# Asking for the first expert's weights during the recurrence, in a gated linear attention followed by a top-2 mixture of experts

## The chip, the core and the metric

The kernel runs on one core of one Trainium2 chip. The metric is device time in microseconds (us); the time of a kernel is the median of its runs. Engines are named as in the profile: PE is the matmul engine (PEld its weight loads), DVE the vector engine, ACT the scalar engine, POOL is GpSimd, and SP the engine whose queue issues most of the transfers here.

## The reference

An attention recurrence over 4 batches, 8 heads, 768 steps and a head dimension of 48, and then a router with 8 experts over the 3072 rows of 384 that it makes:

```python
for t in range(S):
    state = alpha[:, :, t, :, None] * state + einsum('bhd,bhe->bhde', k[:, :, t], v[:, :, t])
    y[:, :, t] = einsum('bhd,bhde->bhe', q[:, :, t], state)
x = y.transpose(0, 2, 1, 3).reshape(3072, 384)
noisy = x @ w_gate + log1p(exp(x @ w_noise)) * noise
top2 = the two largest of each row; top2_w = their softmax
for each expert e, and each row that chose it with weight w:
    out[row] += w * (relu(x[row] @ w1[e]) @ w2[e])      # w1: 384 x 1024, w2: 1024 x 384
```

## The kernel before, in words

All of it is in f32. The first stage is the recurrence, in 24 chunks of 128 rows (6 to a batch); the second is the experts, in 24 pairs of tiles of 128 rows (256 rows for one expert), with three small tiles between them. The order of the instructions on every engine is written out by hand, inside `tc.manual_schedule()`.

**The recurrence.** The loop over n (L1460) runs 23 times, for chunks 0 to 22. Each turn first queues transfers on SP: v of chunk n+2, alpha of n+5, k and q of n+4, and `put_y(n-2)`, which writes finished rows into `x_rows` in DRAM (L1470). Then come 14 pieces in the order ORDER, each for a chunk one to three ahead or behind: transposes of alpha, k and q on PE (`alphas`, `keys`, `queries`, L338), running products on DVE, `scores` (L417), `output` (L461 and L254, whose result ACT copies to yT, L465), and `turn_y(n-1)` (L277), which multiplies yT into rows and router logits, copied by ACT into `y_sb` (L282). Between the pieces, `route` deals out the steps of the router for the six chunks of a unit, and `put_some` writes the chosen rows into `table` in DRAM by indirect transfers of POOL (L169). After the loop, chunk 23 still lacks its `output` and `turn_y`.

**The experts.** A pair goes through: `load_tab` (its part of the table, L1073), `load_w1` and `load_w2` (L946 and L948, 1536 KB each, on SP), `find_rows` on DVE (L1096 to L1108), `gather` (two indirect transfers of POOL from `x_rows` into `x_in`, L936), `turn_x` (six transposes on PE, L1118, copied by ACT to xt, L1119), `sum_x`, `sum_w1` and `sum_w2` on DVE (sums and differences of tiles, so that fewer products are needed, L1124 and L1127), 11 products of the first layer (L1180), 7 of the second (L1187), then `combine` and the indirect write into `out` (L929). Pairs 0 to 7 take the experts 0 to 7 in turn; they need only the rows of the first two units (chunks 0 to 11), so the router's work for units 2 and 3 runs beside them.

**What sets the order.** Each step of pair i has a time, T*i + t with T = 20, and `beside()` adds further steps with times of their own: what is left of the last chunks, of the router and of the table's puts. All are sorted by time (L1410), and the sorted list is the order in which every engine gets its instructions; a time has no other meaning. A pair's first product has t = 0. For the first two pairs EARLY_0 and EARLY_1 replace times by others. Steps with times under -1 are played inside the last turns of the recurrence: `until(t)` runs all steps up to t, and the line

```python
for at, place, t in ((3, 5, -301.0), (3, 9, -300.0), (2, 1, -199.0), (1, 1, -101.0), (1, -1, -100.0)):
    if n == LAST - at:
        chunk.insert(place, lambda t=t: until(t))
```

puts it into turn 23 - at, ahead of piece number `place`. All else follows the loop, in `until(1e9)`.

**Buffers and queues.** w1 and w2 have two buffers each. The two of w1 are used before by `by_chunk` (the router's noise, until turn 2) and `nothing` (zeros to clear the table, until turn 2). SP starts its transfers in the order of the program; each waits for its buffer, for the data, and for the transfer that used its semaphore before, eight places back. POOL's indirect transfers go through a queue of their own.

Of the kernel before, what the change touches and what calls it, by code (L numbers as in the profile page):

```python
# [18 lines left out]
def kernel(  # L19
# [137 lines left out]
    def nothing_in(on):  # L157
        nothing = on.tile([C, KO * F], F32, tag="w1", name="nothing")[:, 0:TROWS // C * 4]
        nc.vector.memset(nothing, 0.0)
        nc.vector.memset(nothing.rearrange("p (r w) -> p r w", w=4)[:, :, 0:1], float(NONE))  # L160
        return nothing

    def clear_table(nothing):
        entries.clear()
        cleared = nc.scalar.dma_start(out=table.bitcast(F32).rearrange("(p r) w -> p (r w)", p=C), in_=nothing)
        entries.append(cleared.ins)
# [48 lines left out]
    def load_router(on):  # L215
        w_r = on["one"].tile([C, NP, 2, E], F32, name="w_r")
        nc.gpsimd.memset(w_r, 0.0)
        place_ident()
        for w, src in enumerate((moe_w_gate, moe_w_noise)):
            for i, part in enumerate(src.rearrange("(j i d) e -> i d j e", i=2, d=D)):  # L220
                nc.sync.dma_start(out=w_r[ds(DP * i, D), :, w, :], in_=part)
        return w_r, load_noise(on)

    def place_router(w_r):
        for odd in range(2):
            nc.gpsimd.tensor_copy(
                out=to_rows.rearrange("p (j o) c -> p j o c", o=2)[:, :, odd, ds((1 - odd) * 2 * D, 2 * E)],
                in_=w_r.rearrange("p (j o) w e -> p j o (w e)", o=2)[:, :, odd])
# [6 lines left out]
    def turn_noise(by_chunk, on):  # L235
        tp = on["tp"].tile([C, E, NT], F32, tag="tp", name="tp")
        for e in range(E):
            nc.tensor.transpose(tp[:, e, :], by_chunk[:, e, :], ident[0:NT, 0:NT])
        nc.scalar.copy(noise.rearrange("p n e -> p e n"), tp)
# [538 lines left out]
    def put_some(n):  # L778
        for place, entry in to_put[:n]:
            put_entries(place, entry)  # L780
        del to_put[:n]
# [262 lines left out]
    def pairs(on):  # L1044
# [180 lines left out]
        def put_pair(i):  # L1225
            for s in range(2):
                put_tile(prev[i % 2][:, s], wheres[i][:, s, 0:1])

        T = 20.0
        EARLY_0 = {"tab": -301.0, "w1": -300.0, "find": -200.0, "gather": -199.0, "w2": -101.0, "turn": -100.0,  # L1230
                   "sum_x": -1.0, "s0": -0.9, "s1": -0.8, "s3": -0.7, "s2": -0.6, "t0": 3.5, "t1": 4.3}
        EARLY_1 = {"tab": -301.0, "find": -0.5, "gather": -0.4, "w1": 0.5, "w2": 5.0}

        def steps(i):
            w = lambda f, a: w1_(i, f, a)
# [2 lines left out]
            after = 3.5 if i > E and divmod(i - E, 2) in [(g, 1) for g in AFTER_GROUP] else 0.0  # L1238
            early = {0: EARLY_0, 1: EARLY_1, E: {"find": T * E - 21.5, "gather": T * E - 21.0}}.get(i, {})
            at = lambda name, t: early.get(name, T * i + t) - T * i  # L1240
# [141 lines left out]
    with ExitStack() as es:  # L1382
        on = pools(es, "")
        shared = on["one"].tile([C, 2 * (NP * (C + 1) + 1) + 4 * NP * C], F32, name="shared")
        (load, load_v, alphas, no_more, products, inverses, keys, scaled_keys, queries, scores, masked, turn_k,
         state, block, output, turn_y, put_y, route, route_on, all_routed, out_of_range, places) = fast_gla(on)
        pair_steps, clear_pairs, T = pairs(on)
        half_steps, clear_halves = small_tiles(on, places, shared)
        LAST = NT - 1
        PUTS = (5.0, 6.3, 7.6, 11.0, 12.3, 16.4, 17.7, 19.0)  # L1390

        def beside():

            at = (-0.95, 4.75, 3.66, 5.25, 6.9, 28.5)
            left = [(at[0], lambda: put_y(LAST - 2)), (at[1], lambda: output(LAST)), (at[2], lambda: turn_y(LAST - 1)),
                    (at[3], lambda: turn_y(LAST)), (at[4], lambda: put_y(LAST - 1)), (at[5], lambda: put_y(LAST)),
                    (6 * T + 5.5, lambda: out_of_range(0)), (6 * T + 18.7, lambda: out_of_range(1))]
            r1, r2, r3 = (5.5, 17.4, 18.7)
            when = lambda *steps: [d * T + t for d, t in steps]
            left += [(t, lambda: route_on(2)) for t in when((0, r2), (0, r2), (0, r3), (1, r1), (1, r2), (1, r3), (2, r1), (2, 12.9), (2, r2))]  # L1400
            left += [(t, lambda: route_on(3)) for t in when((2, r3), (2, r3), (3, r1), (3, r2), (3, r3), (4, r1), (4, r2), (5, 2.9), (5, r1))]
            left += [(t, lambda: route_on(3)) for t in when(*[(8, 3.5), (8, 15.0), (8, r2), (8, r3), (10, 3.5), (10, 15.0), (10, r2), (10, r3)])]
            puts = when(*[(d, t) for d, ts in ((2, (17.7, 19.0)), (3, PUTS), (4, PUTS[:2]), (5, PUTS[1:4] + PUTS[1:]), (6, PUTS[:2]))
                          for t in ts])
            left += [(t, lambda: put_some(1)) for t in puts]
            assert len(puts) == 4 * UC
            return left
# [6 lines left out]
        def until(t):  # L1414
            while work and work[0][0] <= t:
                work.pop(0)[1]()
# [6 lines left out]
        def warm(times):  # L1423
            for _ in range(times):
                nc.tensor.matmul(on["y"].tile([C, NP, C], F32, tag="y", name="y")[:, 0, :], ones, ones, start=True, stop=True)

        with tc.manual_schedule():
            load(0)
            load(1, "a")
            load_v(0)  # L1430
            load(1, "kq")
            warm(3)
            alphas(0)
            products(0)
            inverses(0)
            keys(0)
            scaled_keys(0)
            queries(0)
            alphas(1)
            products(1)  # L1440
            inverses(1)
            load(2)
            warm(2)
            scores(0)
            keys(1)
            no_more(0)
            scaled_keys(1)
            masked(0)
            turn_k(0)
            queries(1)  # L1450
            load_v(1)
            load(3)
            held.extend(load_router(on))
            alphas(2)
            no_more(1)
            load(4, "a")
            state(0)
            products(2)
            no_more(2)
            for n in range(LAST):  # L1460
                pieces = {"keys": lambda: keys(n + 2), "inverses": lambda: inverses(n + 2),
                          "scaled": lambda: scaled_keys(n + 2), "alphas": lambda: alphas(n + 3),
                          "turn_y": lambda: turn_y(n - 1), "turn_k": lambda: turn_k(n + 1),
                          "queries": lambda: queries(n + 2), "products": lambda: products(n + 3),
                          "no_more": lambda: no_more(n + 3), "block": lambda: block(n), "output": lambda: output(n),
                          "state": lambda: state(n + 1), "scores": lambda: scores(n + 1),
                          "masked": lambda: masked(n + 1)}
                names = (FIRST_ORDER if n == 0 else ORDER).split()
                assert sorted(names) == sorted(pieces)
                pieces = [lambda: (load_v(n + 2), load(n + 5, "a"), load(n + 4, "kq"), put_y(n - 2))] + \  # L1470
                    [pieces[name] for name in names]
                chunk = [lambda piece=piece, place=place: (piece(), route(n, place)) for place, piece in enumerate(pieces)]
                last = [lambda: put_some(3)]
                if n == 0:
                    chunk.append(lambda: place_router(held.pop(0)))
                if n == 1:
                    last.append(lambda: held.append(nothing_in(on["two"])))
                if n == 2:
                    chunk.append(lambda: clear_table(held.pop()))
                if n == 2:  # L1480
                    last.append(lambda: (clear_pairs(), clear_halves()))
                if n == 3:
                    last.append(place_slots)
                if n == 2:
                    chunk.insert(NOISE_AT, lambda: turn_noise(held.pop(0), on))
                for at, place, t in ((3, 5, -301.0), (3, 9, -300.0), (2, 1, -199.0), (1, 1, -101.0), (1, -1, -100.0)):
                    if n == LAST - at:
                        chunk.insert(place, lambda t=t: until(t))
                for piece in chunk + last:
                    piece()  # L1490

            until(1e9)
            assert not to_put and all_routed()
# [43 lines left out]
```

## Time and profile before

| | |
|---|---|
| median of 3 runs | 673.34 us (672.64 to 673.82) |
| the profiled execution: its time | 707.68 us |
| its span, first to last instruction | 706.0 us |
| mean granted clock of PE | 0.973 |
| PE busy | 665.5 us, 94% of the span |
| DVE, ACT, POOL busy | 458.5, 271.2, 313.0 us |
| moved by DMA | 105.63 MB, 150 GB/s on average |
| last `scores` of the recurrence on PE | starts at 159.40 us |
| first product of the first pair on PE | starts at 163.28 us |
| last matmul | ends at 697.0 us |

A line of the timeline gives start and duration in us, the engine, the line of the kernel, the operation, the tile written and the tile read, and in brackets how long the engine stood idle before it and what ended that. "SPq" is the queue of SP; the duration there is that of issuing a transfer, not of moving the data. A line of the windows gives, for a stretch of time, the busy time of PE, PEld, DVE, ACT and POOL with the number of their instructions, the granted clock of PE, the share of the DMA engines' time that is used, and GB/s. Names leave buffer numbers out, so both weights are called `w<-in_moe_w_dram`; L946 is a w1 and L948 a w2.

### The profile page before, as it was taken

How to read it: one execution, taken by the hardware profiler on the slowest of the kernel's cores; microseconds unless marked ns; L12 is line 12 of the kernel's file. 1: busy time of each engine (PE TensorE's matmuls, PEld its weight loads, DVE VectorE, ACT ScalarE, POOL GpSimd, SP SyncE). 2: the span in 40 equal slices, each digit the busy share in tenths (PEclk: the TensorE clock that was granted, in tenths of full speed). 3: DMA queues.
4: the chain of work that ended last, by engine and by line, in shares of the span. 5: the costliest groups of instructions: out<-in, count | busy, mean ns of one | idle time of the engine just before them, and what ended most of it. 6: DMA issues, size and time to landing. Idle time of an engine off the chain costs nothing. (4 is left out here: it accounts for less than half of the span.)

```text
span 706.0 us, 14849 instructions
## 1 busy us (share of the span) xinstructions
PE 665.5 (94%) x5605; PEld 636.4 (90%) x5605; DVE 458.5 (65%) x1081; ACT 271.2 (38%) x582; POOL 313.0 (44%) x420
## 2 busy tenths in 40 slices
PE   8999999998999697976999999999999999999994
PEld 6898899998999597975999999999999999998894
DVE  8678889876787465753658677646575565756532
ACT  4666676653433223312233333323333333333320
POOL 5252784873225633672341433443354234641231
PEclk9999999999999888996999999999999999999998
DMA  9998889849555453572520438427453364720111
GB/s 155 161 199 147 143 137 184 151 134 369 193 190 193 129 176 117 173 207 56 216 70 23 165 107 294 143 67 271 155 171 125 123 225 141 249 67 17 45 54 44
DMA packets 144181, 105.63 MB, mean 150 GB/s; under 512 B 109255, under 2 KB 131410, under 8 KB 144100
## 3 DMA queue, kind: packets, MB, share of 16 engines
q1 hardware_dynamic: 131716, 80.37, 44.0%
q0 software_dynamic: 12240, 23.80, 10.8%
q8 instruction: 47, 0.77, 0.5%
q10 hardware_dynamic: 144, 0.41, 0.1%
q14 instruction: 34, 0.28, 0.1%
HBM read 94.99 MB, written 14.86 MB: 156 GB/s over the span
## 5 line engine op out<-in xcount | busy, mean ns | idle before, releaser
L936 POOL DMA_INDIRECT x_in<-x_rows,where x48 | 53.0, 1104 | 170.0 <-PE h_ps L1187 82.4
L1180 PE MATMUL sc<-xs,ws 128*128 128x128 f32 x576 | 76.5, 283 | 4.8 <-ACT m L1258 2.0
L929 POOL DMA_INDIRECT out_dram<-prev,where x48 | 50.9, 1060 | 61.1 <-DVE prev L1208 38.5
L1180 PEld LDWEIGHTS sc<-xs,ws 128*128 128x128 f32 x576 | 70.7, 197 | 6.4 <-ACT m L1258 2.8
L1180 PE MATMUL sc<-xt,w 128*128 128x128 f32 x576 | 75.8, 284 | 0.0
L1180 PEld LDWEIGHTS sc<-xt,w 128*128 128x128 f32 x576 | 73.0, 201 | 0.0
L1191 ACT ACTIVATE h<-h 128x512 f32<-128x512 f32 x72 | 45.4, 631 | 69.8 <-DVE h L1127 69.5
L921 POOL DMA_INDIRECT prev<-out_dram,where x48 | 52.6, 1097 | 43.3 <-DMA out_dram<-prev,where 22.3
L1187 PE MATMUL o_ps<-wt,hx 128*128 128x192 f32 x384 | 70.3, 326 | 0.0
L1127 DVE TENSOR_TENSOR h<-sc,m 128x512 f32<-128x512 f32 x48 | 33.1, 691 | 55.9 <-PE sc L1180 46.2
L1187 PEld LDWEIGHTS o_ps<-wt,hx 128*128 128x128 f32 x384 | 63.7, 190 | 0.0
L169 POOL DMA_INDIRECT table<-entry,place_u x48 | 53.8, 1120 | 15.8 <-issue 15.1
L1180 PE MATMUL sc<-xs,w 128*128 128x128 f32 x384 | 50.9, 287 | 4.3 <-DVE h L1127 4.3
L1180 PEld LDWEIGHTS sc<-xs,w 128*128 128x128 f32 x384 | 46.3, 197 | 7.8 <-DVE h L1127 6.3
L396 POOL TENSOR_TENSOR k_P<-k_P,over 128x512 f32<-128x512 f32 (+1 forms) x25 | 28.9, 1158 | 43.0 <-DVE over L378 17.6
L1180 PE MATMUL h_ps<-xt,w 128*128 128x128 f32 x384 | 47.7, 278 | 0.0
L1196 ACT ACTIVATE o<-o_ps,tab 128x192 f32<-128x192 f32 x23 | 9.6, 419 | 98.3 <-PE o_ps L1187 81.4
L338 PE MATMUL tp<-ident,ins 128*128 128x128 f32 x288 | 43.4, 286 | 3.1 <-DMA ins<-in_alpha_dram 1.8
L1180 PEld LDWEIGHTS h_ps<-xt,w 128*128 128x128 f32 x384 | 45.5, 194 | 0.1
L1127 DVE TENSOR_TENSOR h<-h_ps,m 128x512 f32<-128x512 f32 x24 | 16.6, 690 | 43.8 <-PE h_ps L1180 25.1
L1180 PE MATMUL sc<-xt,ws 128*128 128x128 f32 x192 | 29.2, 298 | 12.8 <-issue 12.8
L422 DVE COPY_PREDICATED shared<-upto,sc 128x512 f32<-128x512 uint32 x48 | 32.5, 733 | 13.3 <-PE sc L417 13.0
(257 smaller groups left out, 1440.3 us busy)
## 6 DMA issues: line engine op xcount, KB each, us to landing
w<-in_moe_w_dram SPq DMA_DIRECT2D x30, 1536.0 KB
ins<-in_alpha_dram SPq DMA_DIRECT2D x24, 192.0 KB
ins<-in_k_dram SPq DMA_DIRECT2D x24, 192.0 KB
ins<-in_q_dram SPq DMA_DIRECT2D x24, 192.0 KB
vt<-in_v_dram SPq DMA_DIRECT2D x24, 192.0 KB
x_rows<-y_sb SPq DMA_DIRECT2D x24, 192.0 KB
ins<-in_moe_w_dram SPq DMA_DIRECT2D x3, 1536.0 KB
shared<-in_moe_w_dram SPq DMA_DIRECT2D x3, 1536.0 KB
```

Of the source, the lines that this page charges most:

```text
L169: put = nc.gpsimd.indirect_dma_start(out=table, out_offset=bass.IndirectOffsetOnAxis(ap=place, axis=0), in_=entry, in_offset=None, bounds_ ...
L338: nc.tensor.transpose(tp[:, j, :], src[:, 2 * j:2 * j + 2, :], ident)
L396: nc.gpsimd.tensor_tensor(c["k"][:, at], c["k"][:, at], over[:, at, 1:CB], op=ALU.mult)
L422: nc.vector.copy_predicated(MTs[n % 2][:, i], mask_upto, sc)
L921: get = nc.gpsimd.indirect_dma_start(out=rows.bitcast(U32), out_offset=None, in_=out.bitcast(U32), in_offset=bass.IndirectOffsetOnAxis(ap= ...
L929: put = nc.gpsimd.indirect_dma_start(out=out, out_offset=bass.IndirectOffsetOnAxis(ap=at, axis=0), in_=rows, in_offset=None, bounds_check= ...
L936: nc.gpsimd.indirect_dma_start(out=rows, out_offset=None, in_=x_rows[0:units * UT, :], in_offset=bass.IndirectOffsetOnAxis(ap=at, axis=0), ...
L1127: nc.vector.tensor_tensor(to, p, q, op=ALU.add)
L1180: nc.tensor.matmul(bank[name][:, f, :], W[:, ds(f * C, C)], X, start=new and f == 0, stop=True, skip_group_check=True)
L1187: nc.tensor.matmul(bank[name], H[:, f, :], W[:, f, :], start=new and f == 0, stop=True, skip_group_check=True)
L1191: nc.scalar.activation(t, t if src is None else src, AF.Relu)
L1196: nc.scalar.activation(to, src, AF.Copy, scale=gate(i, s))
```

## The change

- The first expert's w1 is asked for in turn 7 of the recurrence and its w2 in turn 15, at place 9 of each, instead of in turn 20 and turn 22.
- The first two pairs' parts of the table, asked for in turn 20 before, stay in turn 20 but move from place 5 to place 9.
- The second expert's w1 gets the time -0.95 instead of 0.5 and its w2 3.0 instead of 5.0. On SP the order of these stays as it was: `put_y(21)`, w1, w2, `put_y(22)`.
- `turn_y` of the last chunk, 23, gets 6.15 instead of 5.25: on PE it moves behind the product of ws[2] and xs[2], which has 5.4.
- The times of the table's puts are written out one by one and the tuples of `when` are unpacked; the times are the same.

Apart from this, the order of the instructions on PE is the same, and on DVE, ACT and POOL nothing moves. On SP the two weights of the first expert move forward, by 63 and 26 places.

```diff
-        EARLY_0 = {"tab": -301.0, "w1": -300.0, "find": -200.0, "gather": -199.0, "w2": -101.0, "turn": -100.0,
+        EARLY_0 = {"tab": -300.0, "w1": -410.0, "find": -200.0, "gather": -199.0, "w2": -405.0, "turn": -100.0,
                    "sum_x": -1.0, "s0": -0.9, "s1": -0.8, "s3": -0.7, "s2": -0.6, "t0": 3.5, "t1": 4.3}
-        EARLY_1 = {"tab": -301.0, "find": -0.5, "gather": -0.4, "w1": 0.5, "w2": 5.0}
+        EARLY_1 = {"tab": -300.0, "find": -0.5, "gather": -0.4, "w1": -0.95, "w2": 3.0}
...
-            at = (-0.95, 4.75, 3.66, 5.25, 6.9, 28.5)
+            at = (-0.95, 4.75, 3.66, 6.15, 6.9, 28.5)
             left = [(at[0], lambda: put_y(LAST - 2)), (at[1], lambda: output(LAST)), (at[2], lambda: turn_y(LAST - 1)),
                     (at[3], lambda: turn_y(LAST)), (at[4], lambda: put_y(LAST - 1)), (at[5], lambda: put_y(LAST)),
...
-                for at, place, t in ((3, 5, -301.0), (3, 9, -300.0), (2, 1, -199.0), (1, 1, -101.0), (1, -1, -100.0)):
+                for at, place, t in ((16, 9, -410.0), (8, 9, -405.0), (3, 9, -300.0), (2, 1, -199.0), (1, 1, -101.0), (1, -1, -100.0)):
                     if n == LAST - at:
                         chunk.insert(place, lambda t=t: until(t))
```

More of the change, by code (lines that the diff above doesn't have):

```diff
@@ L1389 @@
         LAST = NT - 1
-        PUTS = (5.0, 6.3, 7.6, 11.0, 12.3, 16.4, 17.7, 19.0)
         def beside():
-            at = (-0.95, 4.75, 3.66, 5.25, 6.9, 28.5)
+            at = (-0.95, 4.75, 3.66, 6.15, 6.9, 28.5)
             left = [(at[0], lambda: put_y(LAST - 2)), (at[1], lambda: output(LAST)), (at[2], lambda: turn_y(LAST - 1)),
@@ L1399, in beside @@
             when = lambda *steps: [d * T + t for d, t in steps]
-            left += [(t, lambda: route_on(2)) for t in when((0, r2), (0, r2), (0, r3), (1, r1), (1, r2), (1, r3), (2, r1), (2, 12.9), (2, r2))]
-            left += [(t, lambda: route_on(3)) for t in when((2, r3), (2, r3), (3, r1), (3, r2), (3, r3), (4, r1), (4, r2), (5, 2.9), (5, r1))]
+            left += [(t, lambda: route_on(2)) for t in when(*((0, r2), (0, r2), (0, r3), (1, r1), (1, r2), (1, r3), (2, r1), (2, 12.9), (2, r2)))]
+            left += [(t, lambda: route_on(3)) for t in when(*((2, r3), (2, r3), (3, r1), (3, r2), (3, r3), (4, r1), (4, r2), (5, 2.9), (5, r1)))]
             left += [(t, lambda: route_on(3)) for t in when(*[(8, 3.5), (8, 15.0), (8, r2), (8, r3), (10, 3.5), (10, 15.0), (10, r2), (10, r3)])]
-            puts = when(*[(d, t) for d, ts in ((2, (17.7, 19.0)), (3, PUTS), (4, PUTS[:2]), (5, PUTS[1:4] + PUTS[1:]), (6, PUTS[:2]))
-                          for t in ts])
+            puts = when(*((2, 17.7), (2, 19.0), (3, 5.0), (3, 6.3), (3, 7.6), (3, 11.0), (3, 12.3), (3, 16.4), (3, 17.7), (3, 19.0), (4, 5.0), (4, 6.3), (5, 6.3), (5, 7.6), (5, 11.0), (5, 6.3), (5, 7.6), (5, 11.0), (5, 12.3), (5, 16.4), (5, 17.7), (5, 19.0), (6, 5.0), (6, 6.3)))
             left += [(t, lambda: put_some(1)) for t in puts]
```

## The prediction

> **What bounds the kernel now.** I read the page first (PE busy 94% of the span), then the waits and the timeline of PE, then those of the SP queue and POOL around the change of stage. From 24 us on PE has no gap of 1 us until the first expert, and from 174 to 697 us none over 0.6 but for a stretch from 234 to 330 us, of which below. So only what PE waits for is worth time. At the join of the two stages it waits three times. PE's timeline there:
>
> ```profile
> 159.40 1.16 PE L417 MATMUL sc<-q_P,k_P 48*128 48x128 f32 x16
> 161.28 0.55 PE L1118 MATMUL x_ps<-ident,x_in 128*128 128x128 f32 x3 [0.72 <-DMA x_in<-x_rows,where]
> 162.66 0.82 PE L1118 MATMUL x_ps<-ident,x_in 128*128 128x128 f32 x3 [0.84 <-DMA x_in<-x_rows,where]
> 163.28 1.92 PE L1180 MATMUL sc<-xt,w 128*128 128x128 f32 x8
> 164.98 2.54 PE L1180 MATMUL h_ps<-xt,w 128*128 128x128 f32 x16
> ...
> 171.92 1.09 PE L254 MATMUL y<-shared,vt 128*48 128x128 f32 x16
> 173.75 1.15 PE L277 MATMUL h_ps<-to_rows,yT 128*128 128x112 f32 x8 [0.74 <-ACT yT L465]
> 174.73 1.07 PE L1180 MATMUL sc<-xs,ws 128*128 128x128 f32 x8
> ```
>
> Both transposes of the first expert's rows wait for the gather into x_in; the last turn_y waits for ACT's copy yT. The matmuls after the first two waits are slow: eight took 1.92 us, where the same form takes 1.05 at 189.19. The windows of 2 us say why, the granted clock (third column from the right):
>
> ```profile
> 160.00:162.00 2.00, 1.11 (x15) 0.68 (x11) 1.34 (x2) 0.72 (x2) 0.00 (x0) 1.00 1.06 393
> 162.00:164.00 2.00, 1.33 (x7) 1.34 (x8) 0.00 (x0) 0.82 (x2) 0.00 (x0) 0.70 1.07 394
> 164.00:166.00 2.00, 2.00 (x11) 2.00 (x11) 1.90 (x7) 0.58 (x1) 0.00 (x0) 0.50 1.07 401
> ```
>
> The clock record has one stretch of 3.41 us at half speed, from 162.8. DMA (second from the right) is full. The gathers and what SP has issued beside them:
>
> ```profile
> 154.28 1.84 POOL L936 DMA_INDIRECT x_in<-x_rows,where  x1 [3.28 <-DVE where L1107]
> 156.42 1.00 POOL L936 DMA_INDIRECT x_in<-x_rows,where  x1 [0.30 <-DVE S L446]
> ```
>
> ```profile
> 151.58 1.11 SPq L1073 DMA_DIRECT2D tab<-table  x2
> 152.74 0.47 SPq L946 DMA_DIRECT2D w<-in_moe_w_dram  x1
> 153.31 0.42 SPq L199 DMA_DIRECT2D vt<-in_v_dram  x1
> 153.84 2.72 SPq L286 DMA_DIRECT2D x_rows<-y_sb  x2
> 156.62 0.47 SPq L948 DMA_DIRECT2D w<-in_moe_w_dram  x1
> 158.18 1.53 SPq L286 DMA_DIRECT2D x_rows<-y_sb  x1
> 159.80 0.48 SPq L946 DMA_DIRECT2D w<-in_moe_w_dram  x1
> 160.33 1.28 SPq L948 DMA_DIRECT2D w<-in_moe_w_dram  x1
> ```
>
> The gathers landed (the trace's semaphore records) at 161.24 and 162.62: 6.96 and 6.20 us after issue. Gathers with no weight transfer near them, such as 360.63, 380.77 and 460.42, landed after 3.0 to 3.1 us; those with one issued 0.2 to 0.6 us behind them, or already running, after 4.6 to 8.0. The first w1 (152.74) landed at 159.67; the packets of the first gather began at 159.0, when those of that w1 ended. So the first expert's weights make its own rows late.
>
> **What the Trainium skill says.** "DMA: Bandwidth & Descriptors", section "Issuing engines are not separate DMA queues": DMAs of SP and GpSimd run on the same 16 engines and interleave. The trace agrees on the sharing (3.1 against 6 to 7 us), and shows the gather nearly last rather than evenly mixed. "TensorE: Matmul & The Clock Gate", section "What's actually happening": PE's clock halves after an idle window of 3413 ns, and the windows run free of the program. The stretch here is 3413 ns long, but 1.56 us of idle were enough; gaps of 1.41 us (21.1) and 0.98 us (62.5) left the clock full. So whether it halves can differ between executions.
>
> **The change, part by part.**
>
> *The gathers.* The first w1 and w2 leave SP at 152.74 and 156.62, and the second w1 stays behind put_y(21), which waits for y_sb at 158.15: it goes at about 158.6, 2.2 us behind the second gather. Gathers with a weight issued 1.6 to 2.3 us behind them landed after 3.0 to 3.5 us in all 11 places. So the rows land at about 157.4 and 159.5, before scores(23) ends at 160.57. Then six transposes run from 160.57; the first three take 0.55 (to 161.12), ACT's copy 0.48 with 0.04 us before and 0.06 after, and product "a" starts at 161.70 instead of 163.28: -1.58. Bounds 0 and -1.58. Next late would be ws[0] on DVE: second xt copy ends at 162.1, sum_x 1.14 and ws[0] 0.68 make it 164.0, and product "b" wants it at 161.70 + 2.68 = 164.4. That holds.
>
> *The half clock.* From "a" to "c" 1.70 us instead of 0.89 (189.19 to 190.08), and from "c" to "b" 2.38 instead of 1.79: 1.40 us, gone if the gap goes. The unprofiled runs may not have had it in each execution; bounds 0 and -1.40, and I take half, -0.70.
>
> *turn_y(23) at 6.15.* It falls behind product "a" on ws[2] (0.98 us from start to start). yT is copied at 173.11 to 173.69, and that product covers it until 173.99, with its operands long ready: -0.74. If ACT were 0.3 us later the rest would show; bounds 0 and -0.74. Its two copies on ACT come some 0.2 us later, and put_y(23) is due only at 28.5.
>
> *Second expert's w1 and w2.* They lose the two transfers ahead of them. DVE waits 1.16 us for this w1 at 171.88; PE has no wait from that, so 0. The gather of the second expert (168.60 and 170.50, landed 174.75 and 176.33, wanted at 179.32) becomes the next tight place: PE wants it at 176.3 to 175.6, DVE's find_rows ends 1.9 us earlier (xs from 162.15 instead of 164.03), so POOL issues at about 166.7 and 168.6; a w1 and w2 issued together (422.68) landed 6.5 and 12.9 us after, here about 171.5, so the gathers run inside it. At 5.8 to 7.9 us the last lands between 174.4 and 176.5: taken 0, at most +0.5.
>
> *The table rows.* The two tab loads are queued four pieces later, but SP has nothing between, and stands from 144.2 to 151.58 for the table's puts: 0.
>
> *Weights in the recurrence.* Two transfers of 1.5 MB, at 393 to 410 GB/s some 3.9 us each (an estimate from the windows), ahead of the loads of chunk 8 (SP at 63.1) and chunk 16 (at 117.6); POOL's puts into the table run from 82 to 104 and from 125 to 149, outside the first and behind the second. What waits behind is SP's in-order queue: v, alpha, k, q, put. From landing to first use k of chunk 12 has 10.5 us to spare, k of chunks 20 and 22 8.2 and 7.4, alpha of chunks 13 and 21 12.3 and 9.7, v 13 or more. SP itself is idle for 3.4 us at 63 to 66.5 and again before 72.7, 80.3, 124.5 and 130.3, so the delay is worked off before chunks 16 and 17, where k has only 4.7. Cover is that reserve: 0. Upper bound below.
>
> Sum: -1.58 - 0.70 - 0.74 = -3.02. Against its own time the profiled execution (707.68, span 706.0) would give up 3.72 with the whole clock stretch: 703.96. It stands 34 us over the median because of idle PE with no late buffer named and half clock between 234 and 330 us, as in this line of PE's waits at 300 to 332:
>
> ```profile
> PE sc L1180 <- issue: 8.9, 1, 8.9
> ```
>
> Pairs there take 31.3, 29.5, 26.9 and 23.9 us against 20.2 elsewhere, 30.8 in all. The change touches none of it, so I carry the saving to the median: 673.34 - 3.02 = 670.3. From 174 us on PE runs through, so what is saved stays saved.
>
> **Rivals.** (a) The rows stay late: vt's 1024 packets of 192 B and the puts, now first in the queue, hold the gather instead. For it: they ran at 158.5 to 160.5 just ahead of it. Against: issued by 154, they should be through by 156. Only turn_y remains: -0.74, 672.6. (b) The wait moves to the second expert's gather: its +0.5 and a half-clock stretch there of 1.4 leave -1.1: 672.2. Against: the slack above. (c) Slower: w2 in the SP queue at chunk 15 holds k of chunk 20. Behind other weights a w2 took 16.41 us to land (160.33). If k were delayed by so much, PE would stall 16.4 - 8.2 = 8.2, lose half of 3.4 at half clock, and still gain 3.0: +6.9, 680.2. It costs more than the gain from a delay of 9.5 us on. Against: the 3.9 us of engine time, and 80% DMA share between 60 and 90.
>
> **How the numbers follow.** Forecast 0.74, own range 669.0 to 671.6 (bounds of the clock term 669.6 and 671.0, and the spread of the three runs, 0.6 to each side); (a) 0.11; (b) 0.06, half of it inside 0.2%; (c) 0.09. About 0.2% (1.3 us) is what a measurement of this kernel can tell from no change. Faster 0.74 + 0.03 = 0.77, same 0.11 + 0.03 = 0.14, slower 0.09. The range 668.8 to 672.7 takes in the forecast, (a) and (b), and leaves out (c) and a little.
>
> **What would show it.** Right: the x_in transposes of the first expert with no DMA wait and PE's gap below 0.5 us; gather to landing near 3.1 us; no half clock at the join; L277 of the last chunk without its ACT wait; "tp" and L254 in the recurrence without DMA waits after 63 and 118 us. Wrong: a gather landing after 160.6, a DMA wait at L338 in chunks 8 to 22, or a new wait at the second expert's L1118.

## The result, and the profile after

| | before | changed |
|---|---|---|
| median of 22 runs each, taken together | 673.98 us (672.53 to 676.59) | 671.52 us (669.84 to 676.42) |
| ratio of the times, with its 95% interval | | 0.9968 [0.9957, 0.998], or -2.2 us [-2.9, -1.35] |
| the profiled execution: its time, its span | 707.68, 706.0 us | 673.52, 671.9 us |
| mean granted clock of PE | 0.973 | 0.996 |

Faster by about 2.2 us where 3.0 was predicted. The 34 us between the two profiled executions are not the change's: that of before has the idle and half-clock stretches of 234 to 330 us that the prediction set aside, that of after has none. Two of the three sets of runs below fell on chips where every kernel has them, the unchanged one too (it took 700.6 and 701.8 us there), so a ratio is always taken inside one set, and the join of the stages is read from the traces. What makes those stretches is not shown. The ratios leave out runs more than 1.5% above the fastest of the same kernel, and on those two chips, where the times of one kernel lie up to 17.5 us apart, one short run can decide how many are left out (10 of the 22 of w2 after the loop); where it matters the medians of all runs stand beside them.

The recurrence itself begins some 2 us later in the profile of after (ACT's copy of yT of chunk 3 is at 42.66 us instead of 40.70), so I compare by distances. PE at the join, in the timeline of the changed kernel:

```profile
162.35 1.16 PE L417 MATMUL sc<-q_P,k_P 48*128 48x128 f32 x16 [0.24 <-POOL k_P L396]
163.44 0.55 PE L1118 MATMUL x_ps<-ident,x_in 128*128 128x128 f32 x3
164.97 0.55 PE L1118 MATMUL x_ps<-ident,x_in 128*128 128x128 f32 x3 [0.98 <-DMA x_in<-x_rows,where]
165.36 1.06 PE L1180 MATMUL sc<-xt,w 128*128 128x128 f32 x8
166.25 1.95 PE L1180 MATMUL h_ps<-xt,w 128*128 128x128 f32 x16
...
173.69 1.16 PE L1180 MATMUL sc<-xs,ws 128*128 128x128 f32 x8
174.69 1.04 PE L277 MATMUL h_ps<-to_rows,yT 128*128 128x112 f32 x8
```

The first three transposes no longer wait, the second three still do, for 0.98 us, and there is a new wait of 0.24 us for POOL in the last `scores`. The eight products took 1.06 us, not 1.92, and `turn_y` has lost its wait. The windows of 2 us give the granted clock, full throughout (third column from the right):

```profile
160.00:162.00 2.00, 1.97 (x22) 1.45 (x21) 0.97 (x2) 0.35 (x1) 1.89 (x2) 1.00 0.59 184
162.00:164.00 2.00, 1.75 (x21) 1.28 (x19) 0.46 (x1) 1.04 (x3) 1.08 (x4) 1.00 0.90 232
164.00:166.00 2.00, 1.02 (x9) 1.03 (x10) 0.88 (x2) 1.07 (x3) 0.00 (x0) 1.00 1.02 412
```

POOL and the queue of SP there:

```profile
157.94 1.84 POOL L936 DMA_INDIRECT x_in<-x_rows,where  x1 [4.75 <-DVE where L1107]
160.08 1.00 POOL L936 DMA_INDIRECT x_in<-x_rows,where  x1 [0.30 <-ACT lgs L279]
161.11 1.19 POOL L396 TENSOR_TENSOR k_P<-k_P,over 128x512 f32<-128x512 f32 x1
```

```profile
155.33 0.88 SPq L1073 DMA_DIRECT2D tab<-table  x2
156.32 0.41 SPq L199 DMA_DIRECT2D vt<-in_v_dram  x1
156.83 3.86 SPq L286 DMA_DIRECT2D x_rows<-y_sb  x3
160.78 0.39 SPq L946 DMA_DIRECT2D w<-in_moe_w_dram  x1
161.22 0.52 SPq L948 DMA_DIRECT2D w<-in_moe_w_dram  x1
```

The gathers landed 3.88 and 4.85 us after issue (6.96 and 6.20 before). But POOL stood 4.75 us for DVE's `where` instead of 3.28, and the product of running decays for chunk 23 (k_P, L396) is queued behind the late gathers: hence the 0.24 us. So the mechanism came as predicted, and something delayed the gathers' issue. That has a second price: SP started the second expert's w1 at 160.78, 0.70 us behind the second gather, where the prediction had it 2.2 us behind. What that costs is worked out below.

For all runs I use three distances in the trace. The first runs from ACT's copy of yT of chunk 21 to the first product of the first pair; it holds the wait for the rows. The second runs from that product to the first product of the second layer (L1187); it holds the half clock, `turn_y` and the second expert's weights. The third is the least time that k of chunks 20 to 22 had from landing to the copy of its transposes.

| kernel | gathers landed after | to first product | to second layer | least k reserve | half clock at the join |
|---|---|---|---|---|---|
| before | 6.96, 6.20 | 8.30 | 16.81 | 7.4 | 3.41 us |
| before again | 7.11, 6.00 | 7.84 | 15.81 | 7.6 | none |
| before, a third time | 7.25, 6.06 | 8.73 | 15.75 | 7.8 | none |
| changed | 3.88, 4.85 | 8.19 | 14.68 | 1.9 | none |
| changed again | 3.85, 3.43 | 6.86 | 14.71 | 3.8 | none |
| changed, turn_y at 5.25 | 3.91, 3.32 | 6.71 | 15.52 | 3.3 | none |
| turn_y alone | 6.83, 5.64 | 7.82 | 15.89 | 6.9 | none |
| turn_y alone, again | 7.04, 5.65 | 7.50 | 15.97 | 7.6 | none |
| w1 alone, turn 7 | 8.78, 7.38 | 10.16 | 16.27 | 7.0 | 3.41 us |
| w2 alone, turn 15 | 7.25, 6.62 | 10.40 | 17.04 | 0.8 | 3.41 us |
| changed, w2 in turn 9 | 3.91, 3.12 | 6.64 | 14.70 | 4.2 | none |
| the same again | 3.91, 3.35 | 6.69 | 14.71 | 8.1 | none |
| changed, w2 after the loop | 3.92, 4.62 | 7.86 | 14.75 | 6.7 | none |
| changed, w2 fetched twice | 3.95, 3.76 | 7.24 | 14.70 | 1.7 | none |

### The profile page after: what moved, and what is told of

It reads as the page before. It is cut to its first block, busy times and chain, and to the rows that moved or that the text cites. A ratio compares the mean times of both kernels' runs of the same rounds, so it can differ in the third digit from the quotient of the medians.

```text
span 671.9 us, 14849 instructions
## 1 busy us (share of the span) xinstructions
PE 653.7 (97%) x5605; PEld 626.8 (93%) x5605; DVE 459.2 (68%) x1081; ACT 270.9 (40%) x582; POOL 315.0 (47%) x420
## 5 line engine op out<-in xcount | busy, mean ns | idle before, releaser
L1180 PE MATMUL sc<-xs,ws 128*128 128x128 f32 x576 | 73.3, 276 | 0.0
L1180 PE MATMUL sc<-xt,w 128*128 128x128 f32 x576 | 72.2, 275 | 0.0
L1187 PE MATMUL o_ps<-wt,hx 128*128 128x192 f32 x384 | 70.3, 326 | 0.0
L1180 PEld LDWEIGHTS sc<-xt,w 128*128 128x128 f32 x576 | 69.1, 192 | 0.0
L1180 PEld LDWEIGHTS sc<-xs,ws 128*128 128x128 f32 x576 | 68.3, 192 | 0.4 <-issue 0.2
L1187 PEld LDWEIGHTS o_ps<-wt,hx 128*128 128x128 f32 x384 | 63.7, 190 | 0.0
L169 POOL DMA_INDIRECT table<-entry,place_u x48 | 55.3, 1153 | 15.7 <-issue 15.0
L396 POOL TENSOR_TENSOR k_P<-k_P,over 128x512 f32<-128x512 f32 (+1 forms) x25 | 28.9, 1157 | 45.2 <-DVE over L378 14.5
L1180 PE MATMUL sc<-xs,w 128*128 128x128 f32 x384 | 49.2, 281 | 0.0
L1180 PEld LDWEIGHTS sc<-xs,w 128*128 128x128 f32 x384 | 44.7, 191 | 3.6 <-DVE h L1127 1.7
L338 PEld LDWEIGHTS tp<-ident,ins 128*128 128x128 f32 x288 | 33.0, 146 | 8.5 <-ACT ins L356 1.7
```

The lines of the kernel that those rows point to most:

```text
L169: put = nc.gpsimd.indirect_dma_start(out=table, out_offset=bass.IndirectOffsetOnAxis(ap=place, axis=0), in_=entry, in_offset=None, bounds_ ...
L338: nc.tensor.transpose(tp[:, j, :], src[:, 2 * j:2 * j + 2, :], ident)
L396: nc.gpsimd.tensor_tensor(c["k"][:, at], c["k"][:, at], over[:, at, 1:CB], op=ALU.mult)
L1180: nc.tensor.matmul(bank[name][:, f, :], W[:, ds(f * C, C)], X, start=new and f == 0, stop=True, skip_group_check=True)
L1187: nc.tensor.matmul(bank[name], H[:, f, :], W[:, f, :], start=new and f == 0, stop=True, skip_group_check=True)
```

## The experiments

The theory: the weights that SP starts next to POOL's gathers hold the first expert's rows, so taking both away makes the rows early, clears the half clock and leaves `turn_y` as a gain of its own. The rivals: the gain is `turn_y`'s alone; or the transfers in the recurrence take back part of it, through SP's queue and the DMA engines. What each expects of a run is put on record ahead of it.

**turn_y alone**, the kernel before with

```diff
-            at = (-0.95, 4.75, 3.66, 5.25, 6.9, 28.5)
+            at = (-0.95, 4.75, 3.66, 6.15, 6.9, 28.5)
```

> The kernel before with one edit, turn_y of chunk 23 at 6.15. If the product of ws[2] and xs[2] covers ACT's copy: no ACT wait at the last L277, 0.7 us faster than before (ratio 0.9989). Rival, that the wait only moves to a later instruction of PE: 0 (ratio 1.0000), with a new wait of 0.5 us or more between 174 and 180 us.

Measured 1.0005 [0.9983, 1.0027]: the interval takes in both answers, and the trace has to decide. In the timeline of PE the wait has moved two places on, and grown:

```profile
174.07 1.04 PE L277 MATMUL h_ps<-to_rows,yT 128*128 128x112 f32 x8
174.95 1.96 PE L1180 MATMUL sc<-xt,w 128*128 128x128 f32 x16
178.09 2.05 PE L1180 MATMUL sc<-xs,w 128*128 128x128 f32 x16 [1.18 <-DVE h L1127]
```

DVE's timeline in the same kernel has the cause, the second expert's w1:

```profile
174.08 0.69 DVE L1127 TENSOR_TENSOR ws<-w 128x512 f32<-128x512 f32 x1 [1.93 <-DMA w<-in_moe_w_dram]
```

DVE takes its work in order: ws, which waits for w1, stands ahead of the h that PE wants. With `turn_y` at its old place PE lost 0.7 to 0.8 us there anyway and came later. So by the trace this edit alone is worth nothing. The same edit in another set:

> turn_y of chunk 23 at 6.15 alone, once more. From the first run: DVE waits for the second w1, PE gets a wait of about 1.2 us at the product of w(1,1) and xs[3] in place of the 0.74 us at L277, so no gain (ratio 0.9995 to 1.0008). Rival (the wait of the first run was chance): 0.7 us faster, ratio 0.9989.

Measured 0.9969 [0.9936, 1.0001], and 701.96 against 701.76 us as medians of all runs: again both answers fit. The trace repeats the first (1.25 us at the same product; to the second layer 15.97, against 15.75 to 15.81 in the two old kernels without a half clock).

**The change without turn_y**, the changed kernel with

```diff
-            at = (-0.95, 4.75, 3.66, 6.15, 6.9, 28.5)
+            at = (-0.95, 4.75, 3.66, 5.25, 6.9, 28.5)
```

> The changed kernel with turn_y of chunk 23 back at 5.25. If the turn's own worth is the wait of 0.74 us that it covered: an ACT wait of 0.74 us at the last L277 again, 0.7 us slower than the changed kernel. Rival (in the changed kernel something else would have been late anyway, as in the run with the turn alone): same time as the changed kernel.

Measured 0.9981 [0.9974, 0.9989]; the whole change in the same set gave 0.9962 [0.9946, 0.9978], so the two intervals just touch. PE's timeline has the old wait back:

```profile
171.21 1.15 PE L277 MATMUL h_ps<-to_rows,yT 128*128 128x112 f32 x8 [0.74 <-ACT yT L465]
```

To the second layer it is 15.52 instead of 14.71. So inside the change `turn_y` is worth 0.81 us by the traces: its cover there is real, because the second w1 now lands early (DVE has no wait for it in either kernel).

**w1 alone**, the kernel before with

```diff
-        EARLY_0 = {"tab": -301.0, "w1": -300.0, "find": -200.0, "gather": -199.0, "w2": -101.0, "turn": -100.0,
+        EARLY_0 = {"tab": -301.0, "w1": -410.0, "find": -200.0, "gather": -199.0, "w2": -101.0, "turn": -100.0,
...
-                for at, place, t in ((3, 5, -301.0), (3, 9, -300.0), (2, 1, -199.0), (1, 1, -101.0), (1, -1, -100.0)):
+                for at, place, t in ((16, 9, -410.0), (3, 5, -301.0), (3, 9, -300.0), (2, 1, -199.0), (1, 1, -101.0), (1, -1, -100.0)):
```

> The kernel before with one edit: the first w1 in turn 7, while the first w2 stays in turn 22 and turn_y and the second pair's weights as before. If the first w1 alone made the gathers late: the first gather lands after 3 to 4 us, the second, with w2 issued beside it or up to 1 us behind, after 4 to 6 us but still near PE's wish, PE's gap at the join under 0.8 us, 1 to 1.6 us faster than before (ratio 0.9976 to 0.9985). Rival (w2 must go too): the second gather after 6 us or more, gap of 1 us or more, within 0.5 us of before.

Measured 1.0049 [1.0015, 1.0084] where a gain was expected, and 704.02 against 701.76 us as medians of all runs: a miss. SP and PE in its timeline, with POOL's two gathers issued at 156.62 and 158.76:

```profile
155.69 0.99 SPq L286 DMA_DIRECT2D x_rows<-y_sb  x2
156.73 0.48 SPq L948 DMA_DIRECT2D w<-in_moe_w_dram  x1
```

```profile
161.18 1.16 PE L417 MATMUL sc<-q_P,k_P 48*128 48x128 f32 x16
165.44 1.64 PE L1118 MATMUL x_ps<-ident,x_in 128*128 128x128 f32 x6 [3.10 <-DMA x_in<-x_rows,where]
166.91 1.44 PE L1180 MATMUL sc<-xt,w 128*128 128x128 f32 x5
```

With w1 gone, w2 is what runs beside the gathers: it left SP 0.11 us behind the first, and the rows landed after 8.78 and 7.38 us, later than in the kernel before. The gain is not a sum of two halves. One weight beside the gathers is as bad as two; only taking both away frees them.

**w2 alone**, the kernel before with

```diff
-        EARLY_0 = {"tab": -301.0, "w1": -300.0, "find": -200.0, "gather": -199.0, "w2": -101.0, "turn": -100.0,
+        EARLY_0 = {"tab": -301.0, "w1": -300.0, "find": -200.0, "gather": -199.0, "w2": -405.0, "turn": -100.0,
...
-                for at, place, t in ((3, 5, -301.0), (3, 9, -300.0), (2, 1, -199.0), (1, 1, -101.0), (1, -1, -100.0)):
+                for at, place, t in ((8, 9, -405.0), (3, 5, -301.0), (3, 9, -300.0), (2, 1, -199.0), (1, 1, -101.0), (1, -1, -100.0)):
```

> The kernel before with one edit: the first w2 in turn 15, the first w1 still in turn 20, the second pair's weights and turn_y as before. Theory A: the gathers are issued 1.8 us later than before and the first w1 still runs just ahead of them, so slower than before by 1 to 2 us (ratio 1.0015 to 1.003). Rival, that the w2 of turn 15 costs nothing: same as before or up to 0.5 us faster (ratio 0.9992 to 1.0000).

Measured 1.005 [1.0025, 1.0075]. The old w1 still runs next to the gathers (7.25 and 6.62 us), and the price of w2 in turn 15 shows with nothing against it, in PE's timeline of the recurrence and at its end:

```profile
133.66 1.06 PE L338 MATMUL tp<-ident,ins 128*128 128x128 f32 x8 [0.96 <-DMA ins<-in_k_dram]
...
162.31 1.16 PE L417 MATMUL sc<-q_P,k_P 48*128 48x128 f32 x16 [0.24 <-POOL k_P L396]
165.19 0.55 PE L1118 MATMUL x_ps<-ident,x_in 128*128 128x128 f32 x3 [1.72 <-DMA x_in<-x_rows,where]
166.71 0.55 PE L1118 MATMUL x_ps<-ident,x_in 128*128 128x128 f32 x3 [0.97 <-DMA x_in<-x_rows,where]
```

A k waits for its transfer, as rival (c) had it, but for 0.96 us. Then the last put into the table takes 5.50 us to land (3.1 to 3.6 in the old kernels), SP asks for the table's rows 2.1 us later, counted from yT of chunk 21, than in the kernel before, and the gathers follow.

**w2 in turn 9**, far from the end of the recurrence; the changed kernel with

```diff
-                for at, place, t in ((16, 9, -410.0), (8, 9, -405.0), (3, 9, -300.0), (2, 1, -199.0), (1, 1, -101.0), (1, -1, -100.0)):
+                for at, place, t in ((16, 9, -410.0), (14, 9, -405.0), (3, 9, -300.0), (2, 1, -199.0), (1, 1, -101.0), (1, -1, -100.0)):
```

> The changed kernel with the first w2 asked for in turn 9 instead of turn 15. Theory A (the w2 of turn 15 holds back the loads of the last chunks, so that the table's last put lands late and the gathers are issued some 1.8 us later than they could be): loads have 4 us or more to spare again in chunks 20 to 22, the put of 12 lands in 3.4 us instead of 5.0, both gathers land before PE wants them, PE's gap at the join below 0.5 us, 3 us faster than before (ratio 0.9955). Theory B (the gathers are late because the table rows are now asked for at place 9, or for another reason that has nothing to do with w2): as the changed kernel, ratio 0.9968, PE waits 0.5 to 1 us at x_ps.

Measured 0.9988 [0.9965, 1.0011], no answer in time: that set is the noisier kind. In the trace PE has no wait over 0.25 us at the join and the first product comes soonest of all kernels (6.64). Again, next to the change itself and on the chip without the stretches:

> The first w2 in turn 9 once more, now beside the changed kernel. Theory A (w2 in turn 15 makes the gathers late): 1 to 1.7 us faster than the changed kernel in the same call, no PE gap over 0.5 us at the join, first product of the second layer 3.6 us earlier after the fourth chunk than in the kernel before. Rival, that the join's gain is lost again later in the experts: same time as the changed kernel though the join is shorter.

> The changed kernel unchanged, beside the others of this call. All theories: ratio 0.9968 within the interval of the first measurement (0.9957 to 0.998), gathers issued some 1.7 us later against the recurrence than in the kernel before.

Measured 0.9964 [0.9955, 0.9973] for turn 9 and 0.9962 [0.9946, 0.9978] for the change as it is. I had expected a gain of 1 to 1.7 us from turn 9, and none is seen. Nor did the delay of 1.7 us come that was expected of the changed kernel's gathers: they went out 0.8 us later than in the first profile of before. The traces agree with the times: this time the changed kernel's gathers land in time too, and what is left is 0.37 us (0.30 in turn 9), in PE's timeline of the changed kernel again:

```profile
160.88 1.16 PE L417 MATMUL sc<-q_P,k_P 48*128 48x128 f32 x16
161.98 0.87 PE L1118 MATMUL x_ps<-ident,x_in 128*128 128x128 f32 x6
163.22 1.16 PE L1180 MATMUL sc<-xt,w 128*128 128x128 f32 x8 [0.37 <-ACT xt L1119]
```

That is the pace of transpose and copy that the prediction had at the end of its first step. So the 0.98 us in the first profile of the change is something that happens in some executions.

**w2 after the loop**, so that it goes behind the gathers; the changed kernel with

```diff
-        EARLY_0 = {"tab": -300.0, "w1": -410.0, "find": -200.0, "gather": -199.0, "w2": -405.0, "turn": -100.0,
+        EARLY_0 = {"tab": -300.0, "w1": -410.0, "find": -200.0, "gather": -199.0, "w2": -0.94, "turn": -100.0,
-        EARLY_1 = {"tab": -300.0, "find": -0.5, "gather": -0.4, "w1": -0.95, "w2": 3.0}
+        EARLY_1 = {"tab": -300.0, "find": -0.5, "gather": -0.4, "w1": -0.9, "w2": 3.0}
...
-                for at, place, t in ((16, 9, -410.0), (8, 9, -405.0), (3, 9, -300.0), (2, 1, -199.0), (1, 1, -101.0), (1, -1, -100.0)):
+                for at, place, t in ((16, 9, -410.0), (3, 9, -300.0), (2, 1, -199.0), (1, 1, -101.0), (1, -1, -100.0)):
```

> The changed kernel with the first w2 behind put_y(21), just ahead of the second expert's w1; the first w1 stays in turn 7. Theory A: nothing is left in the last half of the recurrence that delays the loads, the gathers are issued as early as in the kernel before and land after 3 to 4 us, PE's gap at the join below 0.5 us, 3 us faster than before (ratio 0.9955); DVE waits 2 us or more for the second w1, PE does not. Theory B: as the changed kernel, ratio 0.9968.

Measured 0.9924 [0.9896, 0.9951], the best ratio of its set; the medians of all runs are 697.36 against 700.63 us, or -3.3 us. The trace of its join explains part of that: 7.86 to the first product, with 0.25 us for POOL's k_P and 0.75 us for the rows, and 22.6 us for both distances together, against 21.3 for w2 in turn 9 and 23.7 to 25.1 for the three traces of before. That is 1.0 to 2.5 us, on a chip where the times of the kernel before lie 13.5 us apart. Whether it beats the change elsewhere was not tried. What was expected of the gathers failed: they went out 1.15 us later than the mean of five executions with the old weights, though no w2 is left in the recurrence and the last put landed after 3.55 us. This time it was the reading of the table: from SP's asking to DVE's first use of the rows took 3.24 us, where the fourteen traces have 1.8 to 3.4, whatever the kernel. In DVE's timeline:

```profile
156.69 0.17 DVE L1096 TENSOR_SCALAR tab<-tab 128x2 f32<-128x2 f32 x1 [1.46 <-DMA tab<-table]
```

So a w2 in turn 15 is not the only thing that makes the gathers late; why the reading of the table varies is open.

**w2 fetched twice** in turn 15, to find the edge of the reserve; nothing is left out:

```diff
+                if i == 0:
+                    load_weights(order_of[i], None, now["w2", i])
```

> The changed kernel with the w2 of turn 15 fetched twice into the same buffer (the suspected cost doubled). Theory A: k of chunks 20 to 22, which has 2 us to spare in the changed kernel, is late by 2 us or more, so PE waits at L338 in the last chunks, the gathers are issued 3 us or more later against the recurrence than before, and the kernel is 3 to 6 us slower than the changed one (ratio 1.001 to 1.006 to before). Rival (w2 in turn 15 is hidden in the reserve of the loads): within 0.5 us of the changed kernel.

Measured 1.0085 [1.0053, 1.0116], +5.7 us. The queue of SP, and then PE in the recurrence:

```profile
118.34 0.44 SPq L948 DMA_DIRECT2D w<-in_moe_w_dram  x1
126.36 0.37 SPq L948 DMA_DIRECT2D w<-in_moe_w_dram  x1
126.83 0.53 SPq L199 DMA_DIRECT2D vt<-in_v_dram  x1
127.45 2.00 SPq L195 DMA_DIRECT2D ins<-in_alpha_dram  x1
129.51 3.15 SPq L195 DMA_DIRECT2D ins<-in_k_dram  x1
```

```profile
135.48 1.09 PE L444 MATMUL o_ps<-vt,k_end 128*64 128x48 f32 x16 [3.87 <-DMA vt<-in_v_dram]
136.50 2.08 PE L417 MATMUL sc<-q_P,k_P 48*128 48x128 f32 x16
```

Between the two, SP waits: both fill the same buffer, the first landed at 126.35, and the second left 0.01 us later. So the run does more than double the traffic; it also holds everything behind it in SP's queue for some 8 us, and which of the two made v late is not separated. v breaks first, not k: it is asked for only two chunks ahead and stands directly behind the weights. The stall of 3.87 us brings 6.8 us of half clock with it, and chunk 21 comes 7.0 us later than in the change, counted from chunk 3. This is rival (c) brought about: one w2 lies inside the reserve, two in a row with a wait between them don't.

**The kernel before, twice more**, one execution each, to see how often the half clock at the join is there.

> The kernel before, profiled again. Its join is in the trace of only one execution, with a half-clock stretch of 3.4 us behind the gap. Theory C (the stretch is not in each execution, so the measured gain is nearer to 2.3 than to 3.7 us): both x_ps waits again, 1.2 to 1.6 us together, with or without the stretch. Rival (the stretch follows each time): half clock from about 122 us after the fourth chunk.

> The kernel before, a third profile, as the one ahead of it: Theory C expects at least one of the two without a half-clock stretch at the join, the rival a stretch in both.

They took 707.09 and 704.53 us, in a set where it has a median of 701.76. Neither has a half clock at the join: the first idled for 0.83 and 0.48 us, the other for 1.72 and 0.40. With the two of `turn_y` alone, which have the same weights in the same places, that makes one execution of the five profiled. Where it is missing, the second expert's w1 shows through to PE even in the old kernel, as in PE's timeline of the first of these:

```profile
178.40 2.05 PE L1180 MATMUL sc<-xs,w 128*128 128x128 f32 x16 [0.24 <-DVE h L1127]
```

## Why the prediction came out as it did

**The gathers, predicted -1.58.** Shown in kind: 3.1 to 4.9 us to land with both of the first expert's weights gone from beside them, 5.6 to 8.8 with one of them or both there. In size, the distance to the first product is 8.04 on average over the five executions with the old weights (7.50 to 8.73), so the one profile of before, with 8.30, was a little worse than most. The prediction's end, 161.70 us, is a distance of 6.72; two of the three executions with the new weights have 6.86 and 6.71, a gain of 1.2 to 1.3. In the third it is 8.19, and nothing is gained. What failed there is the statement that the rows land at 157.4 and 159.5 with the second expert's w1 2.2 us behind them, which took the moment of issue from the kernel before. Counted from yT of chunk 21, the first gather was issued between -0.74 and 0.10 us in the five, at 0.11 and -0.04 in the two, and at 0.76 in the third, while that w1 did not move with it. How close it comes sets how long the second gather takes: 4.85 us with a weight 0.70 us behind it (the first profile of the change), 4.62 with 0.77 (w2 after the loop), 3.76 with 0.97 (w2 twice), 3.1 to 3.4 with 1.36 to 2.28 (four traces). After 3.4 us the second rows would have been there at 163.5, before PE had finished with the first at 163.99, so PE's wait of 0.98 us is this weight's doing (an estimate from these lines).

The prediction's explanation of the old delay was wrong in a detail too: that the gather's packets began when those of w1 ended. They began 5.0 to 5.5 us after issue in each of seven traces, among them w1 alone, where no w1 was left and the w2 beside it had been issued 0.11 us later; without a weight they began 2.5 us after issue (seven traces). In the kernel before that is 159.3 us, not 159.0. Of the gathers with a weight 1.6 to 2.3 us behind them, one landed after 2.9 us; the prediction's 3.0 to 3.5 holds for the rest. Rival (a) came in a small part at most: with the new weights the first gather took 3.85 to 3.95 us in all seven traces instead of 3.1, and PE did not wait for it. That the table is asked for at a later place cost nothing, as predicted: in all traces SP asks the moment the last put has landed.

**The half clock, predicted -0.70 as half of 1.40.** The halving was a chance, and a rarer one: one of five. Where it came, the second distance was 16.81 instead of 15.75 to 15.97, so about 1.0 us and not 1.40, in part because DVE's wait for the second w1 shows where the half clock is gone. A fifth of 1.0 is -0.2. With the gathers this is where the sum was too large. The Trainium skill, "TensorE: Matmul & The Clock Gate", section "What's actually happening", has windows that run free of the program, and the runs fit that: 2.12 us of idle in two parts left the clock full, 1.56 us in two parts didn't.

**turn_y, predicted -0.74.** Measured -0.81 in the trace, and 0.9981 against 0.9962, or 1.3 us, in time. The size held, and the reason given did: the product on ws[2] covers ACT's copy. But it holds only together with another part of the change.

**Second expert's weights, predicted 0.** This step failed. "PE has no wait from that" was read from one profile in which PE had been held up by the half clock and by `turn_y`. Take these away, and DVE's wait for w1 reaches PE: 0.24 and 0.16 us in the two further traces of before, 1.18 and 1.25 with `turn_y` moved. The earlier w1 is worth about 0.2, and without it the 0.81 of `turn_y` would be lost. The worry of rival (b), the second expert's gather, did not come: it landed 3.2 to 5.3 us after issue in the three profiles of the change with and without `turn_y`, and PE does not wait for it.

**Weights in the recurrence, predicted 0.** Right in two of three profiles, and for a wrong reason. "The delay is worked off" did not hold: k of chunks 20 to 22 had 7.4 to 9.0 us to spare before and 1.9 to 2.3 in the first profile of the change. The estimate of 3.9 us is the time of a w2 that has the DMA engines to itself; it landed 7.9 to 8.9 us after issue in the three. What this does to the last put into the table is seen in the 3 us from its issue, DMA share second from the right: of the kernel before,

```profile
148.04:151.04 3.00, 3.00 (x53) 2.82 (x53) 1.65 (x4) 1.33 (x5) 2.94 (x4) 1.00 0.06 7
```

of the changed one,

```profile
150.21:153.21 3.00, 3.00 (x53) 2.79 (x53) 1.63 (x4) 1.85 (x5) 2.97 (x4) 1.00 0.76 157
```

and of w2 alone:

```profile
149.76:152.76 3.00, 3.00 (x53) 2.82 (x53) 1.66 (x4) 1.56 (x5) 2.96 (x4) 1.00 0.92 200
```

In these last two the loads of the recurrence are not through when the put goes, and it took 4.97 and 5.50 us to land. In the other twelve traces the share is 0.02 to 0.31, and it took 3.1 to 3.9, also in the two other profiles with w2 in turn 15 and its loads unaltered (3.86 and 3.52). So the put is late where the loads still run, and of all kernels only those with w2 in turn 15 had that, in two profiles of four. The table's rows wait for the put, `where` for them, the gathers for that, and k_P of chunk 23 stands behind the gathers on POOL. The prediction counted SP's queue and k, and called the tab loads 0 because SP has nothing between; it did not follow the put through the busy DMA engines. The other hole, "v 13 or more", took `output` for v's first use: it is `state` (L444), a chunk earlier. There v of chunk 18 had 8.8 us to spare before and 1.8 in the first profile of the change, and there the doubled w2 broke.

**The sum.** Gathers -1.2 where the rows come in time (-0.8 as the mean of the three), half clock -0.2, turn_y -0.8, second w1 -0.2: -2.4 or -2.0, against -2.2 [-2.9, -1.35] and -2.6 [-3.6, -1.5] measured. Both distances together are 22.2 us on average in the two traces of the change and 24.4 in the three of before. The direction was right because the parts that were held for free stay inside their cover in most of the profiles, and the size was 0.6 to 1.0 too large because of the half clock and the gathers. Part of the near agreement is luck: the gain of the second w1, which was left out, makes up for some of what the half clock and the gathers didn't give. What stays open is why the loads run late in some executions and not in others of the same kernel, why the reading of the table varies, how often either is so in the timed runs, and the ratio of w2 after the loop. A kernel clearly better than the change was not found.

## What to carry to other kernels

A large transfer next to a small one that the critical engine waits for is worth moving, but all of them have to go: take one away, and the next in the queue starts in its place. A wait that costs nothing on an engine off the critical path may only be hidden by a stall that you are about to remove, so cost it again with the stalls gone. And to call a moved transfer free, follow not only the queue that it stands in but everything that shares the DMA engines afterwards, down to the small writes whose landing somebody waits for.

## What the runs showed of the hardware

- An indirect gather of POOL began to move data 2.5 us after issue when no weight was on its way, and 5.0 to 5.5 us after issue beside one of 1.5 MB on SP's queue, whether that had been issued 1.5 us earlier or 0.11 us later.
- A weight issued behind the second gather made it land after 4.85 us when it came 0.70 us behind, and after 3.1 to 3.4 when it came 1.36 to 2.28 us behind.
- A small indirect write into the table landed after 3.1 to 3.9 us with the DMA engines 0.02 to 0.31 busy in the 3 us from its issue, and after 4.97 and 5.50 with 0.76 and 0.92.
- SP's issuing itself can be held back behind a large transfer: the next load of alpha behind w2 in turn 15 took SP 1.97 to 4.21 us in four profiles, where the kernel before shows 0.4 to 0.6 at 118 to 131 us; behind w1 in turn 7 it took 0.53 in the first profile of the change.
- The clock halved after idle of 1.56 us in two parts and of 3.10 in one, and stayed full after 2.12 us in two parts.
